# The order of GpSimd's and ScalarE's weight work inside a block of four steps, in a gated attention and GEGLU kernel

## The chip, the cores and the metric

One core of one Trainium2 chip runs the whole program. The metric is the device time of one execution in microseconds (us), taken as the median of several runs. Five engines run their own queues of instructions and wait for each other by semaphores: PE (TensorE, the matrix products), DVE (VectorE), ACT (ScalarE), POOL (GpSimd) and SP (SyncE, which here issues all DMAs).

## The reference

For 2048 tokens of 576 features two branches are computed and mixed by a gate per token:

```python
x = A_x
g = _sigmoid((x * gate_w).sum(-1, keepdims=True))
a = _A_ref(x, A_wq, A_wk, A_wv, A_wo, A_beta)
b = _B_ref(x, B_w_gate, B_w_up, B_w_down)
return g * a + (1 - g) * b
```

Branch A is attention with 32 heads of 18 features in four segments of 512 tokens, with a causal softmax inside a segment and a recurrent memory across segments. Branch B, on which the change acts, is `(gelu(x @ w_gate) * (x @ w_up)) @ w_down` with 4608 hidden features. All numbers are float32.

## The kernel before, in words

Every float32 product is made of float16 products: each operand is scaled and split into a high word (`AF.Copy` on ACT, which rounds) and a low word (the rest, a subtraction on POOL), and PE adds high*high, high*low and low*high. The gate and up products are besides arranged as a Strassen-like scheme, so that PE multiplies sums of weight tiles, which POOL forms first.

The hidden features are cut into 36 tiles `f` of 128. Two tiles make a **block** `fb` (18 blocks), and a block has four **steps** `i4` = 0 to 3: two tiles times two pairs of token segments. The loop runs 72 steps `v` = 4 `fb` + `i4`. Each step also carries the attention of two of 64 units (scores, exponentials, probabilities, values) and eight of the 32 down products of the block before. Inside `tc.manual_schedule` the order of the code is the order of each queue of PE, ACT, DVE and POOL; SP's order is chosen by the scheduler.

What the change and the prediction speak of, with the names in the trace:

- `sums_g(f)` (L401 to L405): five POOL additions in place on the loaded tile `raw`, that form the sums of gate and up weights of tile `f`.
- `scale_g`, `scale_up` (L304, L310): POOL scales `raw`. `scale_d(f)` (L425): POOL scales the loaded down tile `rawd`.
- `high_g(f, b)` and `low_g(f, b)` (L411 on ACT, L417 on POOL): the split of half `b` of tile `f` into `pairg`, in two parts. `high_d`, `low_d` (L429 on ACT, L433 on POOL): the split of the down tile into `paird`.
- `nest_sums`, `nest_high`, `nest_low` (L324, L332, L337): the same for three small extra tiles of the up weights that one pair of segments needs (names `junk`, and `nu` for the sum that L421 forms); `nested` (L380) multiplies by them.
- `hidden_pair` (L1248 on ACT, L1249 on POOL): the split of the activations, `hh`. `pair_rows` (L1156 on ACT, L1157 on POOL): the split of the probabilities, `ph`, twice a step, after ACT's exponentials (L1146); SP turns `ph` into `pt` by a DMA (L1163), and `values` (L1177) reads it.
- `down(fb, t, n)` (L1222): six matmuls of a down product, into one of two PSUM banks `dn`; the matmuls of the second down tile's low word come last. DVE adds each result to `acc` (L1230).
- `result_low` (L1206 on DVE): the low word of finished attention results, `oh` from `ob` and `oh`, once a block. `hidden` (L1244 on DVE): `gl` from the PSUM banks `G` and `U`, which PE may fill again after it.

In a block the second down tile is scaled, split high and split low in step 3, and the first down product of the next step 0 reads it. The gate and up tiles (`raw`, three buffers) and the down tiles (`rawd`, two buffers) are loaded one block ahead, by SP, as soon as their buffer is free.

Of the kernel before, what the change touches and what calls it, by code (L numbers as in the profile page):

```python
# [13 lines left out]
OP = mybir.AluOpType  # L14
# [4 lines left out]
P = 128  # L19
# [7 lines left out]
NF = F // P  # L27
# [19 lines left out]
def kernel(ctx: ExitStack, tc: tile.TileContext, xs, wqk, wv, wo, wgu, wd, beta, out):  # L47
# [24 lines left out]
    def pair_tile(i):  # L72
        return wts.tile([P, 2, (GB if i % 2 else GN) * P], F16, name=f"pairg{i % 2}", tag=f"pairg{i % 2}", bufs=1)
# [255 lines left out]
    def nest_high(f):  # L329
        if f < NF:  # L330
            r, a, b = nest_part(f)
            act.activation(pair_g[f][:, 0, a:b], r, AF.Copy)  # L332

    def nest_low(f):
        if f < NF:
            r, a, b = nest_part(f)
            pool.tensor_tensor(pair_g[f][:, 1, a:b], r, pair_g[f][:, 0, a:b], OP.subtract)  # L337

    def nest_load(p):
        r = nest_x[p, "r"] = home["a"].tile([P, 10 * P], F32, name="pf", bufs=2)  # L340
        sp.dma_start(r[:, : 2 * L], flat(xs[2 * p, :, 2:4]))
# [35 lines left out]
    def nested(o, f, a, p, b, start=False):  # L377
        w, x = pair_g[f], nest_right(p, b)
        for n, (i, j) in enumerate(((0, 0), (0, 1), (1, 0))):
            pe.matmul(o, w[:, i, a * P : (a + 1) * P], x(j), start=start and n == 0, stop=n == 2, skip_group_check=True)  # L380

    def parts_g(f, b):

        if f >= NF:
            return ()
        if b:
            return ((0, KW, S3), (KW, KW + 4 * P, S2))
        return ((KW, 2 * KW, A11), (2 * P, KW, A22))
# [6 lines left out]
    def sums_g(f):  # L395
        if f >= NF:
            return
        r = raw_g[f]
        g0, g2, u0, u2 = (r[:, o : o + 2 * P] for o in (0, 2 * P, KW, KW + 2 * P))
        g4, u4 = r[:, 4 * P : KW], r[:, KW + 4 * P :]  # L400
        pool.tensor_tensor(g2, g0, g2, OP.add)  # L401
        pool.tensor_tensor(g0, u0, g0, OP.subtract)
        pool.tensor_tensor(u0, g2, u0, OP.subtract)
        pool.tensor_tensor(u2, u2, u0, OP.subtract)
        pool.tensor_tensor(g4, u4, g4, OP.subtract)  # L405

    def high_g(f, b):
        if f < NF and not b:
            pair_g[f] = pair_tile(f)
        for p in parts_g(f, b):  # L410
            act.activation(spot(f, *p, 0), raw_g[f][:, p[0] : p[1]], AF.Copy)  # L411
            if b and f % 2 == 0 and f and p[0] == 0:
                nest_high(f)

    def low_g(f, b):
        for p in parts_g(f, b):
            pool.tensor_tensor(spot(f, *p, 1), raw_g[f][:, p[0] : p[1]], spot(f, *p, 0), OP.subtract)  # L417
            if b and f % 2 == 0 and f and p[0] == 0:
                nest_low(f)
                s3 = nest_w[f + 1] = nest_u[NP][:, NL : NL + P]  # L420
                pool.tensor_tensor(s3, raw_g[f + 1][:, KW + 3 * P : KW + 4 * P], nest_w[f][:, P : 2 * P], OP.subtract)  # L421

    def scale_d(f):
        r = raw_d[f]
        pool.tensor_scalar(r, r, scl[f // 2 + 1][0][:, 1:2], None, OP.mult)  # L425

    def high_d(f):
        t = pair_d[f] = home["d"].tile([P, 2, D], F16, name="paird", tag="paird", bufs=4)
        act.activation(t[:, 0], raw_d[f], AF.Copy)  # L429

    def low_d(f):
        t = pair_d[f]
        pool.tensor_tensor(t[:, 1], raw_d.pop(f), t[:, 0], OP.subtract)  # L433
# [635 lines left out]
    with tc.tile_pool(name="keep", bufs=2, side="right", reuse_waits="tile") as kp, ExitStack() as tail:  # L1069
# [206 lines left out]
        def weights_first(fb, i4):  # L1276
            n0 = 2 * fb
            if i4 == 0 and fb:
                scale_g(n0 + 1)
            if i4 == 1 and fb:  # L1280
                sums_g(n0 + 1)
            if i4 == 2 and fb:
                scale_g(n0 + 2)
                scale_d(n0)
            if i4 == 3 and fb:
                sums_g(n0 + 2)
                scale_d(n0 + 1)

        def weights_high(fb, i4):
            n0 = 2 * fb  # L1290
            high_g(n0 + 1 + i4 // 2, i4 % 2)
            if i4 == 0:
                nest_high(n0 + 1)
            if i4 >= 2:
                high_d(n0 + i4 - 2)

        def weights_low(fb, i4):
            n0 = 2 * fb
            low_g(n0 + 1 + i4 // 2, i4 % 2)
            if i4 == 0:  # L1300
                nest_low(n0 + 1)
            if i4 >= 2:
                low_d(n0 + i4 - 2)

        def weights_load(fb, i4):
            n0 = 2 * fb
# [44 lines left out]
        def step(v):  # L1351
# [14 lines left out]
            end_pair()  # L1366
            if v == 3:
                high_g(2, 1)
                low_g(2, 1)
            if v in (1, 3 + NP):  # L1370
                nest_high_x(NP, v > 1)
            act_squares(v)
# [2 lines left out]
            if fb and p == NP and f % 2 == 0:  # L1375
                u = nest_u[p]
                S = bank("dn", 2)
                n0, n1 = slice(0, NL), slice(NL, L)
                nested(X[:, n1], f, N1, p, "t1", True)
                nested(X[:, n0], f, A_11, p, "b11")  # L1380
                nested(S[:, n0], f, N2, p, "t2", True)
                product(Y, f, A11, x1, 0, 4, True)
                put(2 * k - 1, 3)
                dve.tensor_copy(u[:, n0], X[:, n0])
                dve.tensor_tensor(X[:, n0], Y[:, n0], u[:, n0], OP.add)
                dve.tensor_tensor(u[:, n0], S[:, n0], u[:, n0], OP.add)
                dve.tensor_tensor(u[:, n1], X[:, n1], u[:, n0], OP.add)
                dve.tensor_tensor(X[:, n1], Y[:, n1], u[:, n1], OP.add)
            elif fb and p == NP:
                u = nest_u[p]  # L1390
                halves = lambda t: t.rearrange("p (a b) -> p a b", a=2)
                S = bank("dn", 2)
                nested(S[:, :NL], f, N3, p, "t3", True)
                some(fb - 1, early[:1])
                product(Y, f, A11, x1, 0, 4, True)
                put(2 * k - 1, 3)
                dve.tensor_tensor(u, Y, u, OP.add)
                dve.tensor_tensor(halves(X), S[:, :NL].unsqueeze(1).to_broadcast([P, 2, NL]), halves(u), OP.add)
            else:
                product(X, f, A11, x1, 0, 4, True)  # L1400
                put(2 * k - 1, 3)
                dve.tensor_copy(Y, X)
# [58 lines left out]
            if v == 0 or fb > 1 and i4 == 1:  # L1461
                if not fb:
                    scales(fb + 1)
                scales_out(fb + 1)
                if fb:
                    scale_up(2 * fb + 3)
                else:
                    nest_form(NP)
            if on(k - 2) and on(k):
# [10 lines left out]
            if v == 5:  # L1480
                scales(2)
                scales_out(2)
                scale_up(5)
            product(Y, f, S1, t, 0, 2)
            rest(Y, f, G4, x2_, (0,) if fb else (0, 1))
            if fb:
# [326 lines left out]
```

## Time and profile before

| | us |
|---|---|
| median of 3 runs (1565.99 to 1567.05) | 1566.31 |
| the profiled execution | 1566.07 |
| its span, first to last instruction | 1564.3 |
| one block of four steps (window 480.07 to 553.14) | 73.07 |
| PE busy in it | 72.88 |
| POOL busy in it | 65.21 |
| ACT busy in it | 61.99 |
| DVE busy in it | 57.43 |

The granted clock of TensorE is 1.00 in every slice. A row of the timeline gives the start in us, the duration, the engine and the line of the kernel, what is written and read, and how many equal instructions the row holds; in brackets stands how long the engine was idle before it and what ended that. A matmul's end is modelled and overlaps the next one, so the distance from one start to the next tells what a matmul costs. "LDWEIGHTS" (PEld) is the load of a matmul's stationary operand.

### The profile page before, as it was taken

Reading aid. Unit: us, or ns where it says so; the run is one execution under the profiler, and the core shown is the slowest. Engines: PE = TensorE matmul, PEld = TensorE weight load, DVE = VectorE, ACT = ScalarE, POOL = GpSimd, SP = SyncE. Lnnn points to the kernel's source line nnn. Section 1 sums busy time; section 2 is a strip of 40 time slices with the busy share of each in tenths; the row PEclk is TensorE's granted clock in tenths of the full one; section 3 lists DMA queues with packets and bytes.
Section 4 is the critical chain, followed back from the end, with each engine's and each line's share of the span. In section 5 each row is a group of like instructions: output and inputs, shape, how many; then the busy total and the mean of one; then the engine's idle time right before and its main releaser. Section 6 shows DMA issues by size and latency. Waiting matters only on the chain.

```text
span 1564.3 us, 33336 instructions
## 1 busy us (share of the span) xinstructions
PE 1555.5 (99%) x12042; PEld 939.8 (60%) x12043; DVE 1198.3 (77%) x3111; ACT 1184.2 (76%) x2035; POOL 1292.5 (83%) x1309
## 2 busy tenths in 40 slices
PE   9999999999999999999999999999999999999999
PEld 5665655555565555556555555656555556555577
DVE  6788975777878777778787787878787878787665
ACT  7567544888888888887888888888887888876421
POOL 3545776989898989898898989898989898898697
PEclk9999999999999999999999999999999999999999
DMA  7533341787878698978878998989797989884654
GB/s 240 208 131 122 126 136 38 123 135 125 136 128 154 117 144 123 148 122 134 134 132 128 135 139 134 146 122 158 123 139 127 153 118 145 128 136 90 132 111 137
DMA packets 472452, 209.55 MB, mean 134 GB/s; under 512 B 427616, under 2 KB 437344, under 8 KB 471776
## 3 DMA queue, kind: packets, MB, share of 16 engines
q1 hardware_dynamic: 472288, 207.44, 73.7%
q8 instruction: 94, 1.54, 0.4%
q14 instruction: 70, 0.57, 0.1%
HBM read 91.51 MB, written 27.26 MB: 76 GB/s over the span
## 4 chain that ended last, share of the span: by engine, by line
PE 54%; POOL 26%; ACT 12%; issue 6%; DVE 2%; DMA 1%; SPq 0%; POOLq 0%; DVEq 0%
PE dn L1222 13%; PE U L1262 11%; POOL ph L1157 5%; PE V L1262 5%; POOL hh L1249 5%; POOL raw L304 4%; POOL rawd L425 3%; ACT pf L1146 3%; POOL pairg L417 3%; ACT L1146 3%; PE st L440 3%; PE G L1262 2%; PE dn L447 2%; PE pv L1177 1%; ACT gl L1252 1%
## 5 line engine op out<-in xcount | busy, mean ns | idle before, releaser
L1222 PE MATMUL dn<-paird,hh 128*128 128x288 f16 x3396 | 478.8, 286 | 3.2 <-POOL paird L433 3.0
L1157 POOL TENSOR_TENSOR ph<-pf,ph 128x512 f16<-128x512 f32 (+1 forms) x256 | 353.9, 1404 | 114.8 <-ACT ph L1156 108.0
L1262 PEld LDWEIGHTS <-pairg 128*128 128x128 f16 x2820 | 264.0, 98 | 279.0 <-issue 18.0
L1222 PEld LDWEIGHTS <-hh 128*128 128x128 f16 x3456 | 332.1, 98 | 151.9 <-issue 24.5
L1230 DVE SCALAR_TENSOR_TENSOR acc<-dn,ev,acc 128x288 f32<-128x288 f32 x534 | 274.5, 515 | 57.9 <-PE dn L1222 48.0
L1146 ACT ACTIVATE pf<-pf,mb,esc 128x512 f32<-128x512 f32 (+3 forms) x512 | 293.0, 642 | 5.8
L1262 PE MATMUL U<-xt,pairg 128*128 128x512 f16 x864 | 209.9, 379 | 0.0
L417 POOL TENSOR_TENSOR pairg<-raw,pairg 128x640 f16<-128x640 f32 (+2 forms) x144 | 176.5, 1242 | 2.7 <-ACT pairg L411 2.5
L1249 POOL TENSOR_TENSOR hh<-gl,hh 128x512 f16<-128x512 f32 x144 | 164.5, 1163 | 11.5 <-ACT hh L1248 11.5
L1156 ACT ACTIVATE ph<-pf 128x512 f16<-128x512 f32 (+1 forms) x256 | 172.4, 720 | 0.0
L1133 DVE CUSTOM_DVE_ANT_0 pf<-st,mask 128x512 f32<-128x512 f32 (+1 forms) x256 | 157.2, 614 | 0.0
L1262 PE MATMUL U<-x,pairg 128*128 128x512 f16 x636 | 154.6, 379 | 0.1
L411 ACT ACTIVATE pairg<-raw 128x640 f16<-128x640 f32 (+2 forms) x144 | 89.4, 646 | 75.2 <-POOL raw L405 55.6
L1449 DVE COPY gl<-U 128x512 f32<-128x512 f32 x72 | 49.6, 689 | 115.8 <-POOL hh L1249 78.0
L1252 ACT ACTIVATE gl<-gl,sc 128x512 f32<-128x512 f32 x144 | 96.6, 715 | 34.8 <-DVE gl L1491 18.5
L1133 DVE CUSTOM_DVE_ANT_0 pf<-dn,mask 128x256 f32<-128x256 f32 (+1 forms) x192 | 67.2, 375 | 69.0 <-PE dn L1130 68.9
L304 POOL TENSOR_SCALAR raw<-raw,sc 128x640 f32<-128x640 f32 x72 | 118.7, 1661 | 0.0
L1262 PE MATMUL G<-x,pairg 128*128 128x512 f16 x456 | 110.8, 379 | 0.0
L1262 PE MATMUL V<-xt,pairg 128*128 128x512 f16 x432 | 105.7, 381 | 0.0
L1262 PE MATMUL V<-x,pairg 128*128 128x512 f16 x432 | 104.8, 378 | 0.0
L1143 ACT ACTIVATE mb<-mx,esc 128x4 f32<-128x4 f32 x128 | 37.3, 291 | 79.1 <-DVE mx L1133 79.1
L1248 ACT ACTIVATE hh<-gl 128x512 f16<-128x512 f32 x144 | 82.6, 615 | 16.1 <-DVE gl L1244 16.1
(354 smaller groups left out, 2913.8 us busy)
## 6 DMA issues: line engine op xcount, KB each, us to landing
raw<-in_wgu_dram SPq DMA_DIRECT2D x36, 640.0 KB
rawd<-in_wd_dram SPq DMA_DIRECT2D x36, 288.0 KB
qk<-stage SPq DMA_DIRECT2D x36, 256.0 KB
qt<-qk SPq DMA_DIRECT2D x128, 72.0 KB
kt<-qk SPq DMA_DIRECT2D x128, 72.0 KB
vp<-vstage SPq DMA_DIRECT2D x16, 296.0 KB
vt<-vp SPq DMA_DIRECT2D x16, 296.0 KB
qt<-qk SPq DMA_DIRECT2D x128, 36.0 KB
```

The costliest lines, as they stand in the source:

```text
L304: pool.tensor_scalar(r, r, scl[f // 2][0][:, 0:1], None, OP.mult)
L411: act.activation(spot(f, *p, 0), raw_g[f][:, p[0] : p[1]], AF.Copy)
L417: pool.tensor_tensor(spot(f, *p, 1), raw_g[f][:, p[0] : p[1]], spot(f, *p, 0), OP.subtract)
L1133: dve.tensor_tensor_reduce(prob[a][:, COL[qi] : COL[qi + 1]], out[qi], mask[:, L - (qi + 1) * P :], 1.0, -3e38, OP.add, OP.max, mx[a][:, q ...
L1146: act.activation(r, r, AF.Exp, bias=b[:, qi : qi + 1], scale=esc[:, 0, c : c + 1])
L1156: act.activation(h[:, 0, cols], p[:, cols], AF.Copy)
L1157: pool.tensor_tensor(h[:, 1, cols], p[:, cols], h[:, 0, cols], OP.subtract)
L1222: pe.matmul(o[:, :NH], hh[:, a, q * P : (q + 1) * P], w[:, b, n * NH : (n + 1) * NH], start=i == 0, stop=i == 5)
L1230: dve.scalar_tensor_tensor(av, o[:, :NH], ev, av, OP.mult, OP.add)
L1249: pool.tensor_tensor(hh[:, 1], t, hh[:, 0], OP.subtract)
L1252: act.activation(t, o, AF.Gelu_apprx_tanh, scale=scl[f // 2][0][:, 2 + c : 3 + c])
L1262: pe.matmul(o, w[:, i, (a + k) * P : (a + k + 1) * P], x[:, b + k], start=start and k == 0 and i == 0 and b == h, stop=k == 1 and i == 1, ...
```

## The change

Nothing is added or removed: the same instructions stand in another order on POOL, ACT and PE, and with them two loads on SP.

- `scale_d` of both down tiles moves from the starts of steps 2 and 3 to the middle of step 1, behind `scale_up`.
- `sums_g` of the block's odd tile moves from the start of step 1 to step 0, behind `nest_low`.
- In step 3 the high and the low split of the second down tile (`high_d`, `low_d`) move between the two parts of `high_g` and `low_g`, ahead of the nested tiles; the one more nested sum (`s3`, L421 before) is now `nest_third` and comes last.
- In the step's nested products the two halves of bank `G` are filled in the other order.
- In the first block (steps 1, 3 and 5 of the loop) the same calls stand in the new places.

On POOL, in step 3 of a block: `rawd` is the down tile, `pairg_7929` and `junk` the gate, up and nested weights, `nu` the third sum, `ph` the probabilities. Before:

```order
L425 TENSOR_SCALAR rawd<-rawd,sc 128x576
L1157 TENSOR_TENSOR ph<-pf,ph 128x512
L1157 TENSOR_TENSOR ph<-pf,ph 128x768
L417 TENSOR_TENSOR pairg_7929<-raw,pairg_7929 128x640
L337 TENSOR_TENSOR pairg_7929<-junk,pairg_7929 128x384
L421 TENSOR_TENSOR nu_2688<-raw,junk 128x128
L417 TENSOR_TENSOR pairg_7929<-raw,pairg_7929 128x512
L433 TENSOR_TENSOR paird<-rawd,paird 128x576
```

The same place with the change (the line numbers are those of the changed kernel, 8 to 10 higher here; L441 is `low_d`, L427 `low_g`, L343 the third sum):

```order
L1165 TENSOR_TENSOR ph<-pf,ph 128x512
L1165 TENSOR_TENSOR ph<-pf,ph 128x768
L427 TENSOR_TENSOR pairg_7930<-raw,pairg_7930 128x640
L441 TENSOR_TENSOR paird<-rawd,paird 128x576
L337 TENSOR_TENSOR pairg_7930<-junk,pairg_7930 128x384
L427 TENSOR_TENSOR pairg_7930<-raw,pairg_7930 128x512
L343 TENSOR_TENSOR nu_2688<-raw,junk 128x128
```

The scaling is gone from this step, and the low word of the down tile stands fourth instead of eighth.

On POOL, from the middle of step 0 into step 1 of the next block (`hh` are the activations, `ob` a buffer that is cleared). Before:

```order
L417 TENSOR_TENSOR pairg_8465<-raw,pairg_8465 128x384
L337 TENSOR_TENSOR pairg_8465<-nu_2688,pairg_8465 128x128
L1157 TENSOR_TENSOR ph<-pf,ph 128x512
L1157 TENSOR_TENSOR ph<-pf,ph 128x768
L1112 MEMSET ob 128x288
L1249 TENSOR_TENSOR hh_2613<-gl,hh_2613 128x512
L1249 TENSOR_TENSOR hh_2614<-gl,hh_2614 128x512
L401 TENSOR_TENSOR raw<-raw 128x256
L402 TENSOR_TENSOR raw<-raw 128x256
L403 TENSOR_TENSOR raw<-raw 128x256
L404 TENSOR_TENSOR raw<-raw 128x256
L405 TENSOR_TENSOR raw<-raw 128x128
```

With the change (L407 to L411 are the five sums):

```order
L427 TENSOR_TENSOR pairg_8465<-raw,pairg_8465 128x384
L337 TENSOR_TENSOR pairg_8465<-nu_2688,pairg_8465 128x128
L407 TENSOR_TENSOR raw<-raw 128x256
L408 TENSOR_TENSOR raw<-raw 128x256
L409 TENSOR_TENSOR raw<-raw 128x256
L410 TENSOR_TENSOR raw<-raw 128x256
L411 TENSOR_TENSOR raw<-raw 128x128
L1165 TENSOR_TENSOR ph<-pf,ph 128x512
L1165 TENSOR_TENSOR ph<-pf,ph 128x768
L1120 MEMSET ob 128x288
L1257 TENSOR_TENSOR hh_2613<-gl,hh_2613 128x512
L1257 TENSOR_TENSOR hh_2614<-gl,hh_2614 128x512
```

The five sums now stand ahead of the second pair of probabilities in step 0, instead of behind the activations in step 1.

On SP, in step 3, the load of the next down tile now stands ahead of the load of the next gate and up tile. Before:

```order
L1163 DMA_TRANSPOSE pt<-ph 128x10x128 x2
L236 DMA raw<-in_wgu_dram 128x1280
L242 DMA rawd<-in_wd_dram 128x576
L1091 DMA qt<-qk 36x1x1024
L1092 DMA qt<-qk 18x1024
L1093 DMA kt<-qk 36x1x1024
```

With the change:

```order
L1171 DMA_TRANSPOSE pt<-ph 128x10x128 x2
L242 DMA rawd<-in_wd_dram 128x576
L236 DMA raw<-in_wgu_dram 128x1280
L1099 DMA qt<-qk 36x1x1024
L1100 DMA qt<-qk 18x1024
L1101 DMA kt<-qk 36x1x1024
```

The two loads have changed places; what stands behind them (`qt` and `kt`, the operands of the next attention unit) is where it was. The diff:

```diff
--- before.py
+++ after.py
@@ -336,6 +336,12 @@
             r, a, b = nest_part(f)
             pool.tensor_tensor(pair_g[f][:, 1, a:b], r, pair_g[f][:, 0, a:b], OP.subtract)
 
+    def nest_third(f):
+
+        if f < NF:
+            s3 = nest_w[f + 1] = nest_u[NP][:, NL : NL + P]
+            pool.tensor_tensor(s3, raw_g[f + 1][:, KW + 3 * P : KW + 4 * P], nest_w[f][:, P : 2 * P], OP.subtract)
+
     def nest_load(p):
         r = nest_x[p, "r"] = home["a"].tile([P, 10 * P], F32, name="pf", bufs=2)
         sp.dma_start(r[:, : 2 * L], flat(xs[2 * p, :, 2:4]))
@@ -404,21 +410,23 @@
         pool.tensor_tensor(u2, u2, u0, OP.subtract)
         pool.tensor_tensor(g4, u4, g4, OP.subtract)
 
-    def high_g(f, b):
+    def high_g(f, b, between=lambda: None):
         if f < NF and not b:
             pair_g[f] = pair_tile(f)
+        if f >= NF:
+            between()
         for p in parts_g(f, b):
             act.activation(spot(f, *p, 0), raw_g[f][:, p[0] : p[1]], AF.Copy)
-            if b and f % 2 == 0 and f and p[0] == 0:
-                nest_high(f)
-
-    def low_g(f, b):
+            if p[0] == 0 and b:
+                between()
+
+    def low_g(f, b, between=lambda: None):
+        if f >= NF:
+            between()
         for p in parts_g(f, b):
             pool.tensor_tensor(spot(f, *p, 1), raw_g[f][:, p[0] : p[1]], spot(f, *p, 0), OP.subtract)
-            if b and f % 2 == 0 and f and p[0] == 0:
-                nest_low(f)
-                s3 = nest_w[f + 1] = nest_u[NP][:, NL : NL + P]
-                pool.tensor_tensor(s3, raw_g[f + 1][:, KW + 3 * P : KW + 4 * P], nest_w[f][:, P : 2 * P], OP.subtract)
+            if p[0] == 0 and b:
+                between()
 
     def scale_d(f):
         r = raw_d[f]
@@ -1277,30 +1285,29 @@
             n0 = 2 * fb
             if i4 == 0 and fb:
                 scale_g(n0 + 1)
-            if i4 == 1 and fb:
-                sums_g(n0 + 1)
             if i4 == 2 and fb:
                 scale_g(n0 + 2)
-                scale_d(n0)
             if i4 == 3 and fb:
                 sums_g(n0 + 2)
-                scale_d(n0 + 1)
 
         def weights_high(fb, i4):
             n0 = 2 * fb
-            high_g(n0 + 1 + i4 // 2, i4 % 2)
+            high_g(n0 + 1 + i4 // 2, i4 % 2, lambda: (high_d(n0 + 1), nest_high(n0 + 2)) if i4 == 3 else None)
             if i4 == 0:
                 nest_high(n0 + 1)
-            if i4 >= 2:
-                high_d(n0 + i4 - 2)
+            if i4 == 2:
+                high_d(n0)
 
         def weights_low(fb, i4):
             n0 = 2 * fb
-            low_g(n0 + 1 + i4 // 2, i4 % 2)
+            low_g(n0 + 1 + i4 // 2, i4 % 2, lambda: (low_d(n0 + 1), nest_low(n0 + 2)) if i4 == 3 else None)
             if i4 == 0:
                 nest_low(n0 + 1)
-            if i4 >= 2:
-                low_d(n0 + i4 - 2)
+                sums_g(n0 + 1)
+            if i4 == 2:
+                low_d(n0)
+            if i4 == 3:
+                nest_third(n0 + 2)
 
         def weights_load(fb, i4):
             n0 = 2 * fb
@@ -1366,7 +1373,10 @@
             end_pair()
             if v == 3:
                 high_g(2, 1)
+                nest_high(2)
                 low_g(2, 1)
+                nest_low(2)
+                nest_third(2)
             if v in (1, 3 + NP):
                 nest_high_x(NP, v > 1)
             act_squares(v)
@@ -1376,8 +1386,8 @@
                 u = nest_u[p]
                 S = bank("dn", 2)
                 n0, n1 = slice(0, NL), slice(NL, L)
-                nested(X[:, n1], f, N1, p, "t1", True)
-                nested(X[:, n0], f, A_11, p, "b11")
+                nested(X[:, n0], f, A_11, p, "b11", True)
+                nested(X[:, n1], f, N1, p, "t1")
                 nested(S[:, n0], f, N2, p, "t2", True)
                 product(Y, f, A11, x1, 0, 4, True)
                 put(2 * k - 1, 3)
@@ -1464,6 +1474,8 @@
                 scales_out(fb + 1)
                 if fb:
                     scale_up(2 * fb + 3)
+                    scale_d(2 * fb)
+                    scale_d(2 * fb + 1)
                 else:
                     nest_form(NP)
             if on(k - 2) and on(k):
@@ -1481,6 +1493,8 @@
                 scales(2)
                 scales_out(2)
                 scale_up(5)
+                scale_d(2)
+                scale_d(3)
             product(Y, f, S1, t, 0, 2)
             rest(Y, f, G4, x2_, (0,) if fb else (0, 1))
             if fb:
```

## The prediction

> **What bounds the kernel now.** I read the busy shares first, then the chain of waits, the list of waits, and then the timeline around the one wait on PE that comes back. On the page:
>
> ```profile
> PE 1555.5 (99%) x12042; PEld 939.8 (60%) x12043; DVE 1198.3 (77%) x3111; ACT 1184.2 (76%) x2035; POOL 1292.5 (83%) x1309
> PE 54%; POOL 26%; ACT 12%; issue 6%; DVE 2%; DMA 1%; SPq 0%; POOLq 0%; DVEq 0%
> ```
>
> PE is busy 99% of the span; POOL comes next, with 83%. So only what PE waits for, or what makes PE later in some other way, can move the time, and the change neither adds nor removes an instruction. The list of waits (who <- whom: us in total, times, longest) has one wait of PE that belongs to every block, and it is for the low word of the down tile:
>
> ```profile
> PE dn L1222 <- POOL paird L433: 3.0, 16, 0.2
> ```
>
> The record of the wait is short because matmuls are pipelined. What it costs I take from the starts on PE, at one block's first and third down product:
>
> ```profile
> 763.92 0.65 PE L1222 MATMUL dn<-paird,hh 128*128 128x288 f16 x4
> 764.77 0.40 PE L1222 MATMUL dn<-paird,hh 128*128 128x288 f16 x2 [0.19 <-POOL paird L433]
> 765.01 0.66 PE L1177 MATMUL pv<-vt,pt 128*128 128x37 f16 x20
> ...
> 768.32 0.90 PE L1222 MATMUL dn<-paird,hh 128*128 128x288 f16 x6
> 769.05 0.38 PE L1262 MATMUL G<-x,pairg 128*128 128x512 f16 x1
> ```
>
> Six such matmuls take 769.05 - 768.32 = 0.73 us when nothing holds them, and 765.01 - 763.92 = 1.09 where the last two wait for `paird`. The loss is 0.36 a time, 16 x 0.36 = **5.8 us** in all. Nothing else regular on PE has to do with the moved work.
>
> **What the change takes away.** POOL in step 3 of that block (start, duration, engine, line, operands):
>
> ```profile
> 754.80 0.46 POOL L405 TENSOR_TENSOR raw<-raw 128x128 f32<-128x128 f32 x1
> 755.24 1.73 POOL L425 TENSOR_SCALAR rawd<-rawd,sc 128x576 f32<-128x576 f32 x1
> 756.93 2.77 POOL L1157 TENSOR_TENSOR ph<-pf,ph 128x512 f16<-128x512 f32 x2
> 759.65 1.41 POOL L417 TENSOR_TENSOR pairg<-raw,pairg 128x640 f16<-128x640 f32 x1
> 761.01 0.93 POOL L337 TENSOR_TENSOR pairg<-junk,pairg 128x384 f16<-128x384 f32 x1
> 761.88 0.47 POOL L421 TENSOR_TENSOR nu<-raw,junk 128x128 f32<-128x128 f32 x1
> 762.29 1.18 POOL L417 TENSOR_TENSOR pairg<-raw,pairg 128x512 f16<-128x512 f32 x1
> 763.41 1.30 POOL L433 TENSOR_TENSOR paird<-rawd,paird 128x576 f16<-128x576 f32 x1
> ```
>
> POOL runs these without a gap, and L433 ends at 764.71. With the change the scaling (755.24 to 756.93, 1.69) is gone from the chain and `low_d` follows the first L417. It ends at 759.65 - 1.69 + 1.41 + 1.30, about 760.7. PE wants it at 764.77 - 0.36 = 764.4, so 3.7 us are to spare. Its high word must come in time too, which ACT makes:
>
> ```profile
> 755.29 0.74 ACT L411 ACTIVATE pairg<-raw 128x640 f16<-128x640 f32 x1 [1.86 <-POOL raw L405]
> 757.00 0.68 ACT L429 ACTIVATE paird<-rawd 128x576 f16<-128x576 f32 x1
> 764.02 1.35 ACT L1156 ACTIVATE ph<-pf 128x512 f16<-128x512 f32 x2
> ```
>
> L429 moves up to 755.94, behind the first L411, and is done at 756.6, ahead of `low_d`. The nested and second gate splits are the same three ACT operations in another order; the gelu behind them starts when it did, so it hides this edit at no cost. On POOL the nested low word and the second L417 come later in the order by the 1.30 of `low_d`, and earlier by the 1.69 and, for L417, by the 0.47 of the third sum. Neither ends later than before; if that cover went, each tenth late would be paid once a block. What is late next? Behind L433 stands the first `ph` of step 0, which waits for ACT's L1156 of 764.02. So POOL's next step starts when it did, though PE and DVE come there 0.36 sooner. This decides the collision below.
>
> **Where the moved work goes.** POOL's idle time before the second pair of probabilities, in steps 1 and 0:
>
> ```profile
> 728.51 2.77 POOL L1157 TENSOR_TENSOR ph<-pf,ph 128x512 f16<-128x512 f32 x2 [1.62 <-ACT ph L1156]
> ...
> 777.58 0.42 POOL L337 TENSOR_TENSOR pairg<-nu,pairg 128x128 f16<-128x128 f32 x1
> 782.95 2.77 POOL L1157 TENSOR_TENSOR ph<-pf,ph 128x512 f16<-128x512 f32 x2 [4.94 <-ACT ph L1156]
> ```
>
> The five sums of the odd tile are 751.69 to 755.26 = 3.57 us long in step 3 (their last row is L405's above); in step 0 there are 4.94 idle, so the pair of probabilities at 782.95 isn't delayed. The sums of step 1 stood ahead of its first probabilities, so those can start up to 3.57 sooner. The two scalings, 2 x 1.73 = 3.46, come into step 1 behind `scale_up`, where 1.62 was idle; they need 1.84 of the 3.57 that the sums left, so the pair at 728.51 isn't later either. By these rows no pair of probabilities comes later, and I cost the moves at nothing. If the cover of step 1 is not there, the pair at 728.51 comes 1.84 later, and with it `pt` and at worst the values (L1177) that read it.
>
> SP: the load of the down tile is now issued ahead of that of the gate tile, since `rawd` is free sooner (after `low_d`). The transposes of `ph` ahead and the loads of `qt` and `kt` behind keep their places, so nothing queues behind a longer wait; both loads serve work a block later. I cost it at nothing; if `raw` came late it would show as ACT waiting for a DMA. The swapped halves of the nested products are the same matmuls into the same bank: nothing. The edits in the first block use the same cover once, some tenths either way, inside the spread of the runs (1.06 us).
>
> **What it adds: a collision.** In step 0 POOL was idle from 778.00 on; now it adds there. DVE at that time:
>
> ```profile
> 778.33 1.11 DVE L1230 SCALAR_TENSOR_TENSOR acc<-dn,ev,acc 128x288 f32<-128x288 f32 x2
> 779.37 0.81 DVE L1206 SCALAR_TENSOR_TENSOR oh<-ob,wsc,oh 128x576 f16<-128x576 f32 x1
> 780.09 0.74 DVE L1244 SCALAR_TENSOR_TENSOR gl<-G,sc,gl 128x512 f32<-128x512 f32 x1
> 781.30 0.74 DVE L1244 SCALAR_TENSOR_TENSOR gl<-U,sc,gl 128x512 f32<-128x512 f32 x1
> ```
>
> L1206 reads two tiles that both lie in SBUF. It has taken 0.81 in every block but one, where POOL was late and worked beside it (the group: mean of 836 ns; then DVE, POOL, PE):
>
> ```profile
> L1206 DVE SCALAR_TENSOR_TENSOR oh<-ob,wsc,oh 128x576 f16<-128x576 f32 x16 | 13.4, 836 | 0.0
> ...
> 1217.81 1.26 DVE L1206 SCALAR_TENSOR_TENSOR oh<-ob,wsc,oh 128x576 f16<-128x576 f32 x1
> ...
> 1217.54 0.92 POOL L417 TENSOR_TENSOR pairg<-raw,pairg 128x384 f16<-128x384 f32 x1
> 1218.41 0.94 POOL L337 TENSOR_TENSOR pairg<-nu,pairg 128x128 f16<-128x128 f32 x1
> ```
>
> There it took 1.26, 0.45 more, as if it began 0.81 before its end, at 1218.26: 0.20 before the record of the POOL operation ends (1218.46). And POOL's L337 took 0.94 instead of 0.42. PE felt it, by the starts of V and U:
>
> ```profile
> 779.92 1.47 PE L1262 MATMUL V<-xt,pairg 128*128 128x512 f16 x6
> 782.21 1.03 PE L1262 MATMUL U<-x,pairg 128*128 128x512 f16 x4
> ...
> 1218.36 1.47 PE L1262 MATMUL V<-xt,pairg 128*128 128x512 f16 x6
> 1220.99 1.24 PE L1262 MATMUL U<-x,pairg 128*128 128x512 f16 x5
> ```
>
> V to U is 2.29 in the first and 2.63 in the second: PE lost 0.34 of the 0.45, so 0.11 is slack. What queues behind L1206 on DVE are the copies of `G` and `U` (L1244), which free the banks that PE fills next.
>
> When would L1206 meet the sums? They start when the nested low word ends, at 778.0, and go on 0.80 apart and 0.73 long:
>
> ```profile
> 788.19 0.73 POOL L401 TENSOR_TENSOR raw<-raw 128x256 f32<-128x256 f32 x1
> 788.99 0.73 POOL L402 TENSOR_TENSOR raw<-raw 128x256 f32<-128x256 f32 x1
> ```
>
> So the second runs from 778.8 to 779.5 and lets go at 779.3. L1206 comes at 779.37 - 0.36 = 779.0, in the middle of it, and waits 0.3. Less the 0.11 of slack PE loses 0.19 in each of the 15 blocks with such work: **2.9 us**. The bounds: nothing, if L1206 falls into the gap between two sums or does not wait for them; and 0.60 a block, the whole of what the block of 1217 lost, worked out below. I take 2.9, because the place of L1206 in the second sum follows from rows.
>
> The Trainium skill, "SBUF — State Buffer", section "Who interferes with whom", says that a DVE instruction with two inputs in SBUF contends with a GpSimd instruction that reads SBUF, and that whoever issues first holds the shared ports for its whole length while the other is blocked. It speaks against this change. By that rule the wait would last to the end of the sum and the time come out near 1566.2 (the third case below); by the row of 1217.81, which ends the wait 0.20 earlier, near 1563.4.
>
> **The sum.** 1566.07 (the profiled execution, 0.24 under the median) - 5.8 + 2.9 = 1563.2; on the median of 1566.31 it is **1563.4 us**.
>
> **The rivals.**
>
> Clean: the wait for `paird` goes and L1206 costs PE nothing. 1566.3 - 5.8 = 1560.5. For it: a shift of 0.3 on either engine takes L1206 out of the second sum; against it: the phases follow from rows that repeat each block.
>
> Full hold: L1206 waits until the sum's record ends, 779.50 - 779.01 = 0.49, less 0.11 = 0.38, times 15 = 5.7. That eats the gain: 1566.2. For it: DVE did wait for POOL in the block of 1217; against it: it was let go there 0.20 before the record's end. The rule of the Trainium skill, "SBUF — State Buffer", "Who interferes with whom", is this case.
>
> No gain: another wait of the same size stands where `paird`'s was, or L433 wasn't the last to come: 1566.3. Against it: the bracket at 764.77 names it, and 3.7 us are free behind it.
>
> Slower: each block loses what the block of 1217 lost. The place is step 1 of that block, where PE waits for `acc`, which DVE brings late:
>
> ```profile
> 1230.76 0.21 PE L1130 MATMUL pv<-kt,qt 54*128 54x128 f16 x1
> 1231.17 1.02 PE L1222 MATMUL dn<-paird,hh 128*128 128x288 f16 x7 [0.19 <-DVE acc L1230]
> ...
> 791.98 0.21 PE L1130 MATMUL pv<-kt,qt 54*128 54x128 f16 x1
> 792.13 1.15 PE L1222 MATMUL dn<-paird,hh 128*128 128x288 f16 x8
> ```
>
> 0.41 against 0.15 is 0.26 more, and with 0.34 it makes 0.60; times 15 = 9.0, so 1566.3 - 5.8 + 9.0 = 1569.5. It decides from the point at which L1206 is 0.45 late, or DVE's copies take over 1 us to catch up. Against it: here L1206 would be 0.3 late, and the sums no longer stand in step 1.
>
> **How the numbers follow.** Collision at 1563.4: 0.57 (its own range 1561.5 to 1565.5, from 0.06 to 0.31 a block). Clean: 0.21. Full hold: 0.08. No gain: 0.05. Slower: 0.09. The range reaches from the clean case to the full hold, 1560.2 to 1566.4, and leaves out the slower case and the edges of the others. A measurement of this kernel tells 0.2%, 3.1 us, from no change: faster is below 1563.2, which takes all of the clean case and a little under half of the collision, 0.21 + 0.26 = 0.47. Same: 0.31 + 0.08 + 0.05 = 0.44. Slower, 0.09.
>
> **What the profile after would show.** Right: PE's wait for `paird` is gone; L1206's mean stands near 1.1 us instead of 0.84; POOL's idle before the pair of 782.95 falls from 4.94 to about 1; a block takes 73.07 - 0.36 + 0.19 = 72.9. Clean would be L1206 at 0.81 and 72.7; the slower case PE waits for `acc` in step 1 and 73.3. I would be wrong if the pairs of probabilities came later in step 0 or 1, so that the values wait for `pt`, or if the gate weights came late from the reordered loads.

## The result and the profile after

| | before | with the change |
|---|---|---|
| median, us (10 runs each) | 1565.99 (1565.38 to 1567.05) | 1561.86 (1561.45 to 1562.55) |
| span of the profiled execution | 1564.3 | 1559.9 |
| one block of four steps | 73.07 | 72.76 |

The ratio is 0.9973, with a 95% interval of 0.9964 to 0.9983. The forecast was 1563.4, from 1560.2 to 1566.4. The change saves 4.1 us where 2.9 were forecast.

The page of the changed kernel, PE's busy share and the chain of waits by engine (line numbers are up to 14 higher than before: `down` is L1230, `values` L1185, `pair_rows` L1164 and L1165, `low_g` L427, `high_g` L419, `high_d` L437, `low_d` L441, the third sum L343, `sums_g` L407 to L411, `result_low` L1214, `hidden` L1252):

```profile
PE 1553.9 (100%) x12042; PEld 940.3 (60%) x12043; DVE 1189.2 (76%) x3111; ACT 1179.8 (76%) x2035; POOL 1297.0 (83%) x1309
PE 98%; ACT 1%; DVE 0%; issue 0%; POOL 0%; POOLq 0%
```

POOL had 26% of the chain and ACT 12%; now PE has 98% of it. The list of waits has no wait of PE for `paird` any more. These are PE's rows at the place where it was (start, duration, engine, line, operands):

```profile
763.15 0.90 PE L1230 MATMUL dn<-paird,hh 128*128 128x288 f16 x6
763.89 0.66 PE L1185 MATMUL pv<-vt,pt 128*128 128x37 f16 x20
```

The six matmuls take 763.89 - 763.15 = 0.74 us, where they took 1.09. POOL in step 3 of this block:

```profile
757.18 1.40 POOL L427 TENSOR_TENSOR pairg<-raw,pairg 128x640 f16<-128x640 f32 x1
758.54 1.28 POOL L441 TENSOR_TENSOR paird<-rawd,paird 128x576 f16<-128x576 f32 x1
...
761.77 0.45 POOL L343 TENSOR_TENSOR nu<-raw,junk 128x128 f32<-128x128 f32 x1
763.81 2.76 POOL L1165 TENSOR_TENSOR ph<-pf,ph 128x512 f16<-128x512 f32 x2 [1.59 <-ACT ph L1164]
```

The low word of the down tile ends at 759.82; PE's down product starts 3.3 us later, and its low word is wanted last in it. POOL now waits 1.59 us for ACT before the first probabilities of step 0; before the change it had no gap there.

The forecast's collision is there as well. POOL and then DVE in the middle of step 0:

```profile
776.69 0.42 POOL L337 TENSOR_TENSOR pairg<-nu,pairg 128x128 f16<-128x128 f32 x1
777.07 0.72 POOL L407 TENSOR_TENSOR raw<-raw 128x256 f32<-128x256 f32 x1
777.88 0.73 POOL L408 TENSOR_TENSOR raw<-raw 128x256 f32<-128x256 f32 x1
778.68 1.13 POOL L409 TENSOR_TENSOR raw<-raw 128x256 f32<-128x256 f32 x1
...
781.83 1.16 POOL L1165 TENSOR_TENSOR ph<-pf,ph 128x512 f16<-128x512 f32 x1 [0.80 <-ACT ph L1164]
```

```profile
778.25 0.97 DVE L1214 SCALAR_TENSOR_TENSOR oh<-ob,wsc,oh 128x576 f16<-128x576 f32 x1
779.14 0.74 DVE L1252 SCALAR_TENSOR_TENSOR gl<-G,sc,gl 128x512 f32<-128x512 f32 x1
```

The low word of the result (L1214) takes 0.97 us in place of 0.81. It meets the second sum, as forecast, but 0.37 us into it and not 0.2, so it is held for 0.16 and not for 0.3. The third sum takes 1.13 instead of 0.73, since DVE now goes first. Over all blocks L1214's median is 0.952 (it was 0.808).

Two more differences stand outside the regular blocks. The block that was late for a transfer (at 1212, 73.66 us long, 0.59 more than the others) isn't late any more. And the first full block has a new loss: PE's rows there, in step 1,

```profile
280.51 0.91 PE L1230 MATMUL dn<-paird,hh 128*128 128x288 f16 x6
282.49 0.77 PE L1230 MATMUL dn<-paird,hh 128*128 128x288 f16 x5 [1.06 <-DVE mx L1141]
```

show 1.98 us from the first down product to the second, where 0.74 is the rule. PE waits there for DVE, which is late by two tiny operations of four elements a partition (L268 and L270):

```profile
279.38 1.12 DVE L268 TENSOR_SCALAR pb<-z 128x4 int32<-128x4 int32 x1
280.41 0.16 DVE L269 TENSOR_SCALAR v<-v 128x2 int32<-128x2 int32 x1
280.54 1.56 DVE L270 TENSOR_SCALAR pb<-pb 128x4 int32<-128x4 int32 x1
```

POOL's row beside them is that of the probabilities, which the sums had kept later:

```profile
279.31 2.76 POOL L1165 TENSOR_TENSOR ph<-pf,ph 128x512 f16<-128x512 f32 x2 [1.91 <-ACT ph L1164]
```

Before the change the same chain of DVE stood beside the sums (DVE, then POOL):

```profile
279.20 0.61 DVE L264 TENSOR_SCALAR z<-x,z 128x4 f32<-128x4 f32 x1
279.84 0.17 DVE L268 TENSOR_SCALAR pb<-z 128x4 int32<-128x4 int32 x1
279.92 0.70 DVE L269 TENSOR_SCALAR v<-v 128x2 int32<-128x2 int32 x1
280.54 0.16 DVE L270 TENSOR_SCALAR pb<-pb 128x4 int32<-128x4 int32 x1
...
279.86 0.74 POOL L404 TENSOR_TENSOR raw<-raw 128x256 f32<-128x256 f32 x1
```

So the chain was held there too, by sums of 0.73 us (L264 took 0.61 instead of 0.23, L269 0.70 instead of 0.16); beside the longer pieces of the probabilities (1.17 and 1.64 us) it is held longer, and the next operation of DVE starts at 282.01 instead of 280.71 (the step itself begins 0.07 earlier here than before the change).

The books, by the distances between the same matmul (L1138 into `pv`) in successive steps: the wait for `paird`, 18.60 to 18.25 us a step, 16 x 0.35 = 5.6 saved; the collision, 18.63 to 18.66 on most steps 0, 14 x 0.03 = 0.4 lost; the late block, 0.6 saved; the first full block, 19.47 against 18.25, 1.2 lost. Together 4.6; the spans differ by 4.4.

### The profile page after: what moved, and what is told of

The parts are those of the page before. It is cut to its first block, busy times and chain, and to the rows that moved or that the text cites. A ratio compares the mean times of both kernels' runs of the same rounds, so it can differ in the third digit from the quotient of the medians.

```text
span 1559.9 us, 33354 instructions
## 1 busy us (share of the span) xinstructions
PE 1553.9 (100%) x12042; PEld 940.3 (60%) x12043; DVE 1189.2 (76%) x3111; ACT 1179.8 (76%) x2035; POOL 1297.0 (83%) x1309
## 4 chain that ended last, share of the span: by engine, by line
PE 98%; ACT 1%; DVE 0%; issue 0%; POOL 0%; POOLq 0%
PE dn L1230 27%; PE U L1270 21%; PE V L1270 12%; PE G L1270 6%; PE pv L1185 4%; PE st L448 3%; PE dn L455 2%; PE U L1277 2%; PE G L386 2%; PE G L1282 1%; PE V L1282 1%; PE U L448 1%; PE G L448 1%; PE st L1138 1%; PE st L1667 1%; PE V L1277 1%
## 5 line engine op out<-in xcount | busy, mean ns | idle before, releaser
L1230 PE MATMUL dn<-paird,hh 128*128 128x288 f16 x3396 | 476.5, 286 | 1.1 <-DVE mx L1141 1.1
L1165 POOL TENSOR_TENSOR ph<-pf,ph 128x512 f16<-128x512 f32 (+1 forms) x256 | 353.7, 1403 | 106.1 <-ACT ph L1164 103.0
L1230 PEld LDWEIGHTS <-hh 128*128 128x128 f16 x3456 | 332.1, 98 | 147.4 <-issue 19.6
L427 POOL TENSOR_TENSOR pairg<-raw,pairg 128x640 f16<-128x640 f32 (+2 forms) x144 | 176.1, 1240 | 2.6 <-ACT pairg L419 2.6
L1164 ACT ACTIVATE ph<-pf 128x512 f16<-128x512 f32 (+1 forms) x256 | 172.4, 720 | 0.0
L419 ACT ACTIVATE pairg<-raw 128x640 f16<-128x640 f32 (+2 forms) x144 | 89.1, 645 | 49.5 <-POOL raw L411 30.6
```

Source lines behind the costliest of these rows:

```text
L1164: act.activation(h[:, 0, cols], p[:, cols], AF.Copy)
L1165: pool.tensor_tensor(h[:, 1, cols], p[:, cols], h[:, 0, cols], OP.subtract)
L1230: pe.matmul(o[:, :NH], hh[:, a, q * P : (q + 1) * P], w[:, b, n * NH : (n + 1) * NH], start=i == 0, stop=i == 5)
```

## The experiments

The theory after the result: in step 3 the moved scaling and the earlier split each remove the wait, and either would do alone; what is left is a matter of phase, that is of the moment at which POOL's operations meet those of DVE that they hold. The rivals: that both edits are needed, that the phase came from ACT's new order, that the first block's loss has another cause. All kernels but one start from the changed kernel; the second column is the median, then the ratio to the kernel before with its 95% interval, the block, and the median of the result's low word. The time ahead of the first full block differs by up to 1.04 us between the traces (261.91 to 262.95), so that smaller differences are read from steps and blocks and not from the medians.

| kernel | us | ratio | block | low word |
|---|---|---|---|---|
| the change | 1561.86 | 0.9973 (0.9964 to 0.9983) | 72.76 | 0.95 |
| split_only | 1561.28 | 0.9969 (0.9958 to 0.9981) | 72.73 | 0.81 |
| scale_only (from the kernel before) | 1561.19 | 0.9972 (0.9960 to 0.9983) | 72.73 to 72.80 | 0.81 |
| sums_back | 1561.27 | 0.9970 (0.9959 to 0.9982) | 72.73 to 72.83 | 0.81 |
| act_old | 1561.81 | 0.9972 (0.9961 to 0.9982) | 72.77 | 0.96 |
| scale_back_act | 1564.05 | 0.9987 (0.9979 to 0.9996) | 72.93 | 1.12 |
| clear_1 | 1562.53 | 0.9979 (0.9970 to 0.9988) | 72.82 | 1.01 |
| clear_2 | 1564.71 | 0.9994 (0.9985 to 1.0003) | 72.97 | 1.17 |
| clear_4 | 1561.37 | 0.9969 (0.9958 to 0.9981) | 72.73 | 0.81 |
| clear_11 | 1562.07 | 0.9974 (0.9964 to 0.9984) | 72.73 to 72.85 | 0.81 |
| first_block | 1561.36 | 0.9971 (0.9959 to 0.9982) | 72.77 | 0.95 |
| first_old | 1560.61 | 0.9964 (0.9950 to 0.9978) | 72.77 | 0.96 |
| gap | 1560.06 | 0.9964 (0.9952 to 0.9977) | 72.73 | 0.81 |

### Which edit removes the wait

**split_only**: the down scalings and the odd sums are back, the earlier split stays.

```diff
+            if i4 == 1 and fb:
+                sums_g(n0 + 1)
             if i4 == 2 and fb:
                 scale_g(n0 + 2)
+                scale_d(n0)
             if i4 == 3 and fb:
                 sums_g(n0 + 2)
+                scale_d(n0 + 1)
...
-                sums_g(n0 + 1)
...
-                    scale_d(2 * fb)
-                    scale_d(2 * fb + 1)
...
```

> The changed kernel with the down scalings back at the starts of steps 2 and 3 and the odd sums back in step 1; only the earlier split of the second down tile is left. Theory (the split alone removes the wait, since PE was kept waiting by 0.35 us a block and the split moves by over 2): no wait of PE for paird, a block of 72.72 us, no collision of the result's low word with the sums (0.81 us each), no loss of 1.2 us in step 1 of the first full block. 1566.0 - 16 x 0.35 = 1560.4; 1559.8 if the single late block of the kernel before (0.6 us) goes too. Rival (the scaling must leave step 3 as well): the wait for paird stays in part, 1564 or more.

It has no wait of PE for `paird`, blocks of 72.73 us (but for one of 72.89 and the late one) and no loss in the first full block: the split alone removes the wait. It came out 0.9 us above the 1560.4 of the theory, because the late block did not go but grew: 74.26 us, 1.53 over the rule. A gate load came late there, and with POOL late the result's low word met the splits. The rows of ACT, DVE and PE:

```profile
1207.38 0.74 ACT L95 ACTIVATE junk<-raw 128x640 bf16<-128x640 f32 x1 [2.63 <-DMA raw<-in_wgu_dram]
...
1213.24 2.03 DVE L1214 SCALAR_TENSOR_TENSOR oh<-ob,wsc,oh 128x576 f16<-128x576 f32 x1
...
1215.99 0.82 PE L386 MATMUL G<-x,pairg 128*128 128x256 f16 x6 [0.72 <-DVE gl L1252]
```

**scale_only**: the kernel before, with `scale_d` of both tiles moved to the middle of step 1 and nothing else.

> The kernel before with only the down scalings moved to the middle of step 1; sums and splits where they were. Theory (either edit of step 3 alone ends the wait for paird, since GpSimd is 1.69 us earlier at its low word and only 0.36 was missing): no wait of PE for paird, and the price of scalings and sums standing in step 1 together, 0.85 in the first full block and 0.08 in half of the others, as with the sums back: 1561.3. Rival (the split must also move): the wait stays at 0.2 to 0.36, 1565 or more.

1561.19, and again no wait of PE for `paird`: either edit alone does. The price of scalings and sums standing together in step 1 is there as expected: 0.85 us in the first full block (18.84 and 17.86 in steps 1 and 2), and 0.04 to 0.06 in step 2 of half the other blocks.

**sums_back**: the changed kernel with `sums_g(n0 + 1)` at the start of step 1 again.

> The changed kernel with the odd sums back in step 1; the down scalings stay in step 1 too. Theory (the sums in step 0 cost the collision, 15 x 0.03, and the 1.2 us of the first full block): both go, 1561.9 - 0.4 - 1.2 = 1560.2, the result's low word at 0.81 us. Rival (the space that the sums leave in step 1 is needed for the scalings): the second pair of probabilities in step 1 comes 1.8 us later, the values wait for it, 15 x up to 1.8 on top, 1561 to 1587.

1561.27, at the foot of the rival's range. The collision is gone (0.81). The rival is right about the lateness and wrong about its price. POOL's row of the second probabilities of step 1, here and in the changed kernel:

```profile
584.19 2.77 POOL L1165 TENSOR_TENSOR ph<-pf,ph 128x512 f16<-128x512 f32 x2
...
582.22 2.76 POOL L1165 TENSOR_TENSOR ph<-pf,ph 128x512 f16<-128x512 f32 x2
```

The block begins at 554.20 here and at 553.94 there, so they come 1.7 us later (29.99 against 28.28 from its start). That costs PE 0.07 to 0.10 in step 2 of the first half of the blocks, not 1.8, and 0.9 in the first full block. So the cover that the sums gave up is needed, but most of the lateness is slack.

### What sets the size of the collision

**act_old**: ACT's high word of the down tile last in step 3, as before.

```diff
-            high_g(..., lambda: (high_d(n0 + 1), nest_high(n0 + 2)) if i4 == 3 else None)
+            high_g(..., lambda: nest_high(n0 + 2) if i4 == 3 else None)
...
-            if i4 == 2:
-                high_d(n0)
+            if i4 >= 2:
+                high_d(n0 + i4 - 2)
```

> The changed kernel with ScalarE's order in step 3 as before (the high word of the down tile last again). Theory (the other order of four operations on ScalarE gave it 0.14 us, which brings GpSimd's sums 0.14 sooner in step 0 and so halves the collision): the sums come 0.14 later against the result's low word, which takes 1.09 instead of 0.95 us, PE loses 0.17 instead of 0.03 in 15 blocks: 1561.9 + 2.1 = 1564.0, block 72.9. Rival (the phase has another cause): low word at 0.95 us, 1561.9.

1561.81 and 0.96 us: the theory fell. ACT's order has nothing to do with it. What remained was a wait that the order hid, that of ACT for POOL's scaling in step 3. The list of waits of the kernel before has this pair, but not in that step:

```profile
ACT paird L429 <- POOL rawd L425: 26.2, 18, 3.9
```

These 18 are the waits of step 2 (16 of 1.18 us) and two near the end of the program (3.9 and 3.4 us). The wait in step 3 is short, and only the rows show it. The scaling (L425 at 755.24 in the prediction) ends at 756.97, ACT's split of the down tile starts at 757.00, and ACT's row ahead of it starts 0.65 us earlier:

```profile
756.35 0.61 ACT L411 ACTIVATE pairg<-raw 128x512 f16<-128x512 f32 x1
757.00 0.68 ACT L429 ACTIVATE paird<-rawd 128x576 f16<-128x576 f32 x1
```

In act_old, with the same order but the scaling gone, the same two stand 0.52 apart:

```profile
755.86 0.61 ACT L419 ACTIVATE pairg<-raw 128x512 f16<-128x512 f32 x1
756.38 0.67 ACT L437 ACTIVATE paird<-rawd 128x576 f16<-128x576 f32 x1
```

**scale_back_act**: act_old with `scale_d` back at the starts of steps 2 and 3 as well (sums still in step 0).

> The changed kernel with the down scalings back at the starts of steps 2 and 3, and ScalarE's high word of the down tile last in step 3, as before; the sums stay in step 0. Theory (in the kernel before, ScalarE's high word waited 0.13 us for GpSimd's scaling in step 3; with the scaling gone ScalarE, and GpSimd's sums behind it, come 0.14 sooner, which is why the collision was small): that wait is back, the sums come 0.14 later against the result's low word, which takes 1.09 us instead of 0.95, PE loses 0.17 instead of 0.03 in a block: 1561.9 + 15 x 0.14 = 1564.0, block 72.9. Rival (the scaling has nothing to do with the phase): low word 0.95 us, block 72.76, 1561.9.

1564.05 against 1564.0 expected, block 72.93. ACT waits again, and the sums meet the low word earlier in the sum. The rows of ACT, POOL and DVE:

```profile
756.86 0.61 ACT L419 ACTIVATE pairg<-raw 128x512 f16<-128x512 f32 x1
757.50 0.68 ACT L437 ACTIVATE paird<-rawd 128x576 f16<-128x576 f32 x1
...
779.30 0.73 POOL L408 TENSOR_TENSOR raw<-raw 128x256 f32<-128x256 f32 x1
...
779.53 1.11 DVE L1214 SCALAR_TENSOR_TENSOR oh<-ob,wsc,oh 128x576 f16<-128x576 f32 x1
```

0.64 us from one split to the next, and L1214 comes 0.23 into the sum instead of 0.37. POOL itself is as late here as ACT (its third sum ends at 765.21, the probabilities start at 765.22), so this run alone shows only that with the scaling in step 3 the sums come 0.14 later. The rows of the four kernels speak for ACT: from its first split in step 3 to its first probabilities of step 0 it needs 8.73 us before the change and in scale_back_act, and 8.59 with the change and in act_old, and in all four POOL starts those probabilities 0.69 after ACT does. With the change these two rows of ACT are:

```profile
754.53 0.74 ACT L419 ACTIVATE pairg<-raw 128x640 f16<-128x640 f32 x1 [1.86 <-POOL raw L411]
...
763.12 1.35 ACT L1164 ACTIVATE ph<-pf 128x512 f16<-128x512 f32 x2
```

No run with the sums in step 0 has POOL late there and ACT on time, so the two are told apart by these rows alone.

**clear_1, clear_2, clear_4, clear_11**: the changed kernel with so many clearings of a spare tile of 128x16 ahead of the odd sums, which change nothing but the sums' phase.

```diff
                 nest_low(n0 + 1)
+                for _ in range(4):
+                    pool.memset(pause, 0.0)
                 sums_g(n0 + 1)
```

> The changed kernel with four tiny clearings (128x16) of a spare tile added ahead of the odd sums in step 0 of GpSimd, to bring the sums about 0.18 us later. Theory (the result's low word waits for the sum that it meets until 0.18 us before that sum's record ends, and PE pays what is over 0.11): the wait is 0.14 + 0.18 = 0.32, the low word 1.13 us, PE loses 0.21 in a block instead of 0.03: 1561.9 + 15 x 0.18 = 1564.6, block 72.94. Rival (DVE's lateness costs PE nothing): block 72.76, 1561.9.

> The same with eleven tiny clearings, about 0.5 us. Theory (who comes first holds, so that a later second sum finds the low word at work): the low word falls between the first and the second sum, takes 0.81 us, the second sum waits instead, PE loses nothing: 1561.9 - 15 x 0.03 = 1561.4, block 72.73. Rival (the more delay, the more PE pays): the low word waits 0.6 or more, block 73.2, 1568.

> The changed kernel with one tiny clearing ahead of the odd sums in step 0 (four of them took 0.58 us, so 0.15 each). Theory (the low word is held until 0.18 before the end of the sum it meets; PE pays what is over 0.11): it meets the second sum 0.15 earlier in that sum, waits 0.29, takes 1.10 us, PE loses 0.18 in a block: block 72.90, 1561.9 + 14 x 0.15 = 1564.0. Rival (the block pays 0.03 whatever the place in the sum): 72.76, 1561.9.

> The same with two clearings, 0.29 us. Theory: the low word comes 0.1 us into the second sum, waits 0.43, takes 1.24 us, PE loses 0.32 in a block: block 73.05, 1561.9 + 14 x 0.29 = 1566.0, the gain of the change gone. Rival (so near the start of the sum the low word is let in first): low word 0.81, block 72.73, 1561.4.

The doses were misjudged: the four take 0.58 us and not 0.18, the eleven 1.77. With four, DVE comes between the first and the second sum, which is what was expected of the eleven; POOL and DVE in clear_4:

```profile
777.32 0.73 POOL L407 TENSOR_TENSOR raw<-raw 128x256 f32<-128x256 f32 x1
778.13 1.21 POOL L408 TENSOR_TENSOR raw<-raw 128x256 f32<-128x256 f32 x1
...
777.94 0.81 DVE L1214 SCALAR_TENSOR_TENSOR oh<-ob,wsc,oh 128x576 f16<-128x576 f32 x1
```

The low word takes 0.81, the sum behind it 1.21, and PE pays nothing (72.73). With eleven the low word comes during the clearings and ahead of the first sum, and takes 0.81; but the sums end so late that the second probabilities start at 782.50 without a gap, and step 1 costs 0.03 to 0.12 in the first half of the blocks. With one and two clearings the low word is held longer, 1.01 and 1.17 us, though less than expected (1.10 and 1.24), since these came to less in phase than their number times 0.15. The rows of clear_2:

```profile
778.85 0.73 POOL L408 TENSOR_TENSOR raw<-raw 128x256 f32<-128x256 f32 x1
...
779.02 1.17 DVE L1214 SCALAR_TENSOR_TENSOR oh<-ob,wsc,oh 128x576 f16<-128x576 f32 x1
```

Four kernels give one law. How far into the second sum the low word comes, how long it is held (its duration less 0.81), and what step 0 loses against 18.63:

| kernel | comes at | held | PE loses | held less PE's loss |
|---|---|---|---|---|
| the change | 0.37 | 0.16 | 0.05 | 0.11 |
| clear_1 | 0.31 | 0.22 | 0.10 | 0.12 |
| scale_back_act | 0.23 | 0.30 | 0.19 | 0.11 |
| clear_2 | 0.17 | 0.36 | 0.25 | 0.11 |

(The block around 772 to 846 of each.) "Comes at" and "held" add up to 0.53: DVE is let go 0.53 into a sum of 0.73, that is 0.20 before its record ends. And 0.11 of what DVE is late is free for PE. Both are the prediction's numbers. The other blocks agree: in all 107 holds of the low word, in nine kernels, it is let go 0.19 to 0.20 before POOL's record ends. With 0.20 us less phase, clear_2 gives back 2.9 of the change's 4.1 us, and its interval reaches over 1.

### The first full block

**first_block**: the odd sums in step 1 in that block alone.

```diff
+            if i4 == 1 and fb == 1:
+                sums_g(n0 + 1)
...
-                sums_g(n0 + 1)
+                if fb > 1:
+                    sums_g(n0 + 1)
```

> The changed kernel with the odd sums in step 1 in the first full block alone (block 1), as before. Theory (there two tiny scale operations of VectorE, 128x4, stood against GpSimd's probabilities and took 1.12 and 1.56 us, because the sums no longer stood beside them; PE lost 1.2): step 1 of that block is back at 18.25 us, 1561.9 - 1.2 = 1560.7. Rival (that loss comes from the scalings of the down tiles or from the loads): 1561.9.

1561.36, where 1560.7 was expected. L268 and L270 are back at 0.17 and 0.16, so the sums' place is what made these two slow (L264 and L269 are held instead, as before the change); but now POOL has sums and scalings in that step and is late with the probabilities and the split of the activations. Steps 1 and 2 of the block take 18.84 and 17.87 (18.25 and 17.60 before), 0.86 lost in another way:

```profile
DVE gl L1462 <- POOL hh L1257: 4.9, 1, 4.9
...
PE U L1270 <- DVE gl L1462: 0.4, 1, 0.4
```

**first_old**: in that block the sums and the scalings where they were (as above, with `scale_d` at the starts of steps 2 and 3 for `fb == 1`, and without the two at `v == 5`).

> The changed kernel with sums and down scalings of the first full block (block 1) alone where they were before. Theory (that block loses 1.2 us with the sums moved, 0.85 with only the scalings moved, nothing with neither): step 1 of it 18.25 us, step 2 17.61, 1561.9 - 1.2 = 1560.6. Rival (the loss comes back in the next block, where the places change): 1561.5 or more.

1560.61 against 1560.6 expected; the steps are 18.25 and 17.61. So it takes both moves back to end this loss: with the sums alone back 0.86 stays (first_block), and with the scalings alone back step 1 still takes 19.46 (scale_back_act).

**gap**: first_old with four clearings ahead of the sums.

> The changed kernel with the first full block as before and four tiny clearings ahead of the odd sums in the others, so that the low word falls between two sums: the two losses that the experiments found, taken away together. Theory (they add): 1560.6 - 14 x 0.03 = 1560.2, every block 72.73. Rival (the block around 1208 is late by 0.6 to 1.5 us for a late transfer, as in two of the kernels): 1560.8 to 1561.7.

1560.06, every regular block 72.73 us. The two losses add (1560.2 was expected), and the late block is on time. It is the fastest kernel of the study, by 1.8 us under the change.

## Why the prediction was right, step by step

- **The wait for `paird`: right.** 0.35 a time measured, 0.36 forecast. The split was 3.7 us ahead by the forecast, and its low word did end 3.3 us before the first of the six matmuls started; split_only and scale_only show that either edit was enough.
- **The collision: right in mechanism and place, too large in size**, 0.4 us in all and not 2.9. The step that failed is "POOL's next step starts when it did, though PE and DVE come there 0.36 sooner". The first probabilities of step 0 wait for ACT, as the prediction said, but ACT did not stay: its split of the down tile no longer waits for POOL's scaling, which gave it 0.14, so "the gelu behind them starts when it did" was wrong as well. From its first split to its first probabilities it needs 8.59 us (754.53 to 763.12) instead of 8.73 (755.29 to 764.02). In the frame of step 0 the second sum starts 0.16 sooner than forecast. L1214 comes where it was forecast (step 0 begins 1.12 us earlier in this trace, of which the forecast's 0.36 is the wait: 778.25 + 1.12 - 0.36 = 779.01). Since being held falls off one for one with the phase and the first 0.11 is free, 0.16 of phase took away nearly all of the 0.19 a block. With the scaling back (scale_back_act) the loss is 0.19 to 0.20 in most blocks, the forecast's very number. The prediction's case of a collision began at 0.06 a block, and 0.03 was measured, so by what PE lost this is nearly the clean case. That 1561.86 still lies in the collision's own range (1561.5 to 1565.5) is luck: with the loss of the first full block taken away (first_old) the time is 1560.61, below it. Of the signs, POOL's idle time fell as forecast (0.80, about 1 forecast), while L1214's mean of 0.95 (1.1 forecast) and the block of 72.76 (72.9 forecast) stand between collision and clean.
- **The first blocks "some tenths either way": wrong**, 1.2 us. The prediction priced them by the cover of the other blocks; in that block DVE's scale chain stands at another place, beside the probabilities. The same law of holding that it used for L1206 applies to L268 and L270, but it did not look for other operations of DVE to which it applies.
- **The late block was left out** of the sum: 0.6 us came back there. In split_only, where the load of the down tile goes first too, that block is late still, so that order alone does not end the lateness; and the late transfer is that of the down tile before the change and that of the gate tile in split_only. When the loads are issued may matter: the later of the two goes out 8.6 us ahead of this block before the change and 8.7 in split_only, and 9.9 to 10.4 in the eleven kernels in which the scaling has left step 3 in this block, all of them on time. But scale_back_act issues at 8.7 too and no transfer is late there, so the cause is not shown, and why only this block is late stays open.
- **The moved work at no cost: right** for the regular blocks. Where the sums keep their place beside the scalings, 1.7 us of lateness in step 1 cost 0.04 to 0.10 in half the blocks.
- **The rivals**: clean was 1560.5; gap, which has neither loss, runs at 1560.06. The full hold fails, since no low word was held to the end of POOL's record. No wait of the size of `paird`'s came in its place, so "no gain" fails too. The slower case needed 0.45 of lateness at L1206; clear_2 has 0.36 and gives 1564.71. The errors partly made up for each other, which is luck: the collision was priced 2.5 too high and 0.6 of the late block was left out, while 1.2 of the first full block were left out and the wait was priced 0.2 too high.

## What to carry to other kernels

Before work is moved into an idle stretch of GpSimd, list what VectorE runs there that reads two SBUF tiles, and every small scalar operation on SBUF, and work out the phase to a tenth of a microsecond: in this kernel an operation was held until 0.1 to 0.2 us before the GpSimd record ended, and a shift of 0.2 us cost the larger part of the gain (clear_2). An engine that waits for the moved work gains too, if only 0.1 us; look at the distance of rows as well as at idle times. And price the irregular blocks (the first ones) by their own rows.

## What the runs showed of the hardware

- A hold of VectorE by GpSimd ends before the GpSimd record does, by 0.19 to 0.20 us for the low word, and who comes first goes first: the sum behind the low word took 1.21 us instead of 0.73 in clear_4. The Trainium skill, "SBUF — State Buffer", "Who interferes with whom", has the rule that two SBUF inputs on VectorE contend with a GpSimd instruction that reads SBUF, and that the other is blocked for the whole instruction; the traces agree on who waits, and the wait ends those 0.19 to 0.20 us sooner.
- The hold does not depend on the size of the held operation: two of four elements a partition, which read a single tile, took 1.12 and 1.56 us instead of 0.17 and 0.16, each held until about 0.14 before a piece of the probabilities ended.
- Beside GpSimd's clearings (clear_11) the low word takes its usual 0.81 us. One clearing is only 0.11 us long, less than the 0.20 by which a hold ends early, so this does not show that a long clearing would hold nothing.
